# New cost table for a static order, and the scale matmuls' tile: from a corner of the scores' tile to the transposes' PSUM pool

## The chip, the cores and the metric

The kernel runs on one core of a Trainium2 chip. The metric is the device time of one execution in microseconds (us), the median of several runs. All engines of the core take part: TensorE (PE, matmuls), VectorE (DVE), ScalarE (ACT), GpSimd (POOL) and SyncE (SP, which here only issues DMAs).

## The reference

Attention on q, k, v of shape (4 batches, 8 heads, 576 positions, 64), and a mixture of four experts on what it gives:

```python
scores = q @ k.T / sqrt(64)
scores = where(scores >= max(scores) - tau, scores, -1e9)      # tau = 0.02
attn   = softmax(scores) @ v                                   # per batch and head
x      = attn.transpose(0, 2, 1, 3).reshape(2304, 512)
p      = domain_probs / (domain_probs.sum(-1) + 1e-9)
out    = sum over e of p[:, e] * (relu(x @ w1[e]) @ w2[e])     # w1: 512x1024, w2: 1024x512
```

Inputs and output are float32. Nearly all products are taken as three float16 products (high by high, high by low, low by high), for which each operand is scaled by a power of two and split in two.

## The kernel before, in words

**Attention.** One item is a pair of heads of one batch (`g`) and one block `j` of 128 query rows (`j` = 4 is the 64 rows left over). There are 80 items, 20 for each batch. An item's path: PE writes the scores S of two heads (`emit_qk`, L909 and L915 or L921); DVE copies them with the row's maximum (L968), ACT takes the exponential (L991), POOL the threshold (L983), DVE applies it and sums (L1000). In batch 0 the result is turned on PE (ET, L1020, L1049). In batches 1 to 3 ACT and DVE split it in two float16 parts (L1119, L1125) and SP issues DMA transposes (L1082). Then PE multiplies with V (av, L1232 to L1246), and ACT and DVE write the block X of the experts' input (L1277, L1288).

**Experts.** Experts 0 and 1 run beside the attention. As soon as a block X is there, units of it follow: first layer (L1348), relu and split (ACT L1360 and L1368, POOL L1375), second layer (L1390), result to `acc` (L1407, L1415). Their place in the order of priority is last (1000 and more), so that they fill PE where the attention has nothing ready. Experts 2 and 3 follow in a second stage, with seven products in place of eight (L1584, L1604 to L1632, L1664, L1682). Their weights are prepared from priority 500 on.

**Scales.** Each power of two comes from sums of squares (`squares`, on ACT or DVE), one small matmul with a matrix of ones that adds them over the partitions and spreads the sum (`total`, L453), and five DVE steps on its result (`pow2`, L467 to L486). The matmul's target `au` comes from `chain_tile`: below priority 999 one of two 128-column corners (`am0`, `am1`) of the tile `s_all`, three PSUM banks in which the scores also lie. Columns 704 to 960, the corners, are in the same bank as columns 512 to 576 and 960 to 1024, which belong to the scores. `total` is called for the queries and keys of each pair of heads of batches 1 to 3 (`t_bound`, 12 times), for V of each batch (`v_prep`, 4) and for the weights of experts 0 and 1 (`w_prep`, 2 and 4): 22 in all; the second stage's 8 have tiles of their own (QA).

**Pool `ma`.** Two PSUM tiles of one bank. ET, rp (the reciprocals' spread, batch 0 alone) and av take tiles from it. Tiles of a pool are granted in the order in which they were first named.

**The order.** Nothing is reordered on the chip: each engine runs its instructions in the order in which they were emitted, and `Plan` (L22 to L219) writes that order down while the kernel is built. It plays the program with a cost in ns for each operation, a latency from engine to engine (`LAT`), a delay until a freed tile can be taken (`FREED`), costs for DMAs, and a model of PE's two clocks, and at each moment gives a free engine the ready operation of lowest priority number. The costs set nothing but this order: a cost that is too long puts what depends on it later in its engine's queue than the chip would need. A dependency, also one between two uses of one bank of a tile, becomes a semaphore wait.

Of the kernel before, what the change touches and what calls it, by code (L numbers as in the profile page):

```python
# [21 lines left out]
class Plan:  # L22
# [6 lines left out]
    LAT = {  # L29
        ("PE", "PE"): 0, ("PE", "ACT"): 230, ("DVE", "ACT"): 198, ("ACT", "DVE"): 145,  # L30
        ("PE", "DVE"): 200, ("POOL", "DVE"): 50, ("ACT", "POOL"): 200, ("SP", "PE"): 0,
        ("SP", "ACT"): 0, ("SP", "DVE"): 0, ("SP", "POOL"): 0, ("POOL", "SP"): 70,
    }
    GAP, FILL = 400, 3000
    WINDOW, WARMUP = 3413.0, 4000.0
    warm, cold, work, window, pe_end = True, 0.0, 1e9, 0, 0.0
    FREED, LANES = 150, 8
    START, DONE, HELD = 625, 1000, 877

    def __init__(self):  # L40
        self.ops, self.writer, self.readers = [], {}, {}
        self.slots, self.kinds, self.order, self.users = {}, {}, {}, {}
        self.tiles = {}

# [29 lines left out]
    def reserve(self, u):  # L74
        pool = self.kinds[u[0]][0]
        s = (pool, u)
        if s not in self.users:
            self.users[s] = 0
            self.order[pool].append(u)
        return s  # L80
# [20 lines left out]
    def schedule(self):  # L101
        n = len(self.ops)
# [15 lines left out]
        at = [0.0] * n  # L118
# [17 lines left out]

        now, seq = 0.0, 0
        while True:
            progress = True
            while progress:  # L140
                progress = False
                for e in engines:
                    if free[e] > now:
                        continue
                    skipped = []
                    pick = None
                    h = ready[e]
# [12 lines left out]
                    for u in use:  # L160
                        if u not in granted:
                            pool = self.kinds[u[0]][0]
                            granted.add(u)
                            avail[pool] -= 1
                            head[pool] += 1
# [62 lines left out]
def topk_attention_moe_kernel(  # L228
# [201 lines left out]
    def squares(n, dst, src, junk, r, w, use, prio, on_dve=False):  # L430
        if on_dve:
# [9 lines left out]
        act(  # L441
            n / 0.96 + 200,
            lambda: nc.scalar.activation(
# [6 lines left out]
    def total(n, au, src, r, w, use, prio):  # L450
        pe(
            300,
            lambda: nc.tensor.matmul(pl.t(*au)[:, 0:n], ones, src(), start=True, stop=True),  # L453
# [5 lines left out]
    def pow2(src, s_out, p_out, r, w, use, prio, tmp, au, add=None):  # L459
# [3 lines left out]
        def step(fn, rr, ww, more=()):  # L463
            dve(195, fn, rr, ww, use=use + list(more), prio=prio)

# [179 lines left out]
    def t_turn(g, prio):  # L645
# [12 lines left out]
        for c, n, u in ((0, 1024, ru), (8, 256, tl)):  # L658
            act(
                n / 1.1 + 200,  # L660
                lambda c=c: nc.scalar.activation(
# [4 lines left out]
            dve(  # L666
                n / 0.84 + 80,
                lambda c=c: nc.vector.scalar_tensor_tensor(
# [280 lines left out]
    def item(i):  # L949
# [11 lines left out]
        pe(  # L961
            (1300 if j < 4 else 1150) - 300 * (g >= NP * T32), lambda: emit_qk(pl.t(*su), pl.t(*T), j),
            [("T", g)] if g >= NP * T32 else [("T", g, c) for c in (0, 1024)], [("S", i)], use=[su, T], prio=i,
        )
        for h in heads:

            def cm(h=h):
# [7 lines left out]
            o = dve(  # L975
                890, cm, [("S", i), "tc"] + [("qf", g)] * (g >= NP * T32), [("ss", i, h), ("m", i, h)], use=[su, ssu, mu], prio=i,
            )
        if SK(i) == "S0":
            b_users.append(o)
        for h in heads:  # L980
            gp(
                470,
                lambda h=h: nc.gpsimd.tensor_scalar(  # L983
# [14 lines left out]
            dve(  # L998
                930,
                lambda h=h, col=col: nc.vector.scalar_tensor_tensor(  # L1000
# [14 lines left out]
        for h in heads:  # L1015
# [15 lines left out]
            for hh in range(2 if j == 4 else 0):  # L1031
# [5 lines left out]
            pe(  # L1037
                470, tr, [("E", i, h), "ident"], [("et", i, h)], use=[au, eu], prio=i + 0.2,
            )
# [46 lines left out]
    def spread(i, c0):  # L1086
# [5 lines left out]
        def rec():  # L1092
# [6 lines left out]
        dve(  # L1099
            391, rec, [("ri", i, h) for h in heads], [("ri", i)], use=[ru], prio=i + 0.2,  # L1100
        )
# [13 lines left out]
        for h in heads:  # L1115
# [7 lines left out]
            def lo(h=h):  # L1123
# [6 lines left out]
            act(  # L1130
                767 if j < 4 else 1100, hi, [("E", i, h), ("ri", i)], [("eh", i, h)],
                use=[eu, fu, ru], prio=i + 0.2,
            )
            dve(
                824 if j < 4 else 1159, lo, [("E", i, h), ("ri", i), ("eh", i, h)],
                [("el", i, h)], use=[eu, fu, ru], prio=i + 0.2,
# [20 lines left out]
    def group(gi):  # L1157
# [115 lines left out]
        for Xu, c0, o, c, jj in dest:  # L1273
            key = ("x", Xu, b, jj, pr)
            act(
                c / 1.2 + 210,
                lambda Xu=Xu, c0=c0, o=o, c=c: nc.scalar.activation(  # L1277
# [43 lines left out]
    def unit(name, Xu, xkeys, c0, tiles, u, first, last):  # L1321
# [16 lines left out]
        for f in range(f0, f1):  # L1338
# [3 lines left out]
            def g1(mu=mu, W=W):  # L1342
# [15 lines left out]
            act(  # L1358
                {256: 467, 128: 364}[n],
                lambda mu=mu, hru=hru, f=f: nc.scalar.activation(  # L1360
# [12 lines left out]
            gp(  # L1373
                {256: 850, 128: 536}[n],
                lambda hu=hu, hru=hru: nc.gpsimd.tensor_tensor(  # L1375
# [5 lines left out]
        for i, t in enumerate(tiles):  # L1381
# [22 lines left out]
            if first:  # L1404
                act(
                    571,
                    lambda ou=ou, acc=acc, s=s: nc.scalar.activation(  # L1407
# [121 lines left out]
    def unit7(name, xs, m, tiles, u, last):  # L1529
# [5 lines left out]
        for j in range(2):  # L1535
# [3 lines left out]
            gp(  # L1539
                267,  # L1540
                lambda j=j: nc.gpsimd.tensor_scalar(  # L1541
# [27 lines left out]
        for k in range(4):  # L1569
# [6 lines left out]
            def product(r, a, b, reg=reg, pu=pu, P=P, q=q, k=k):  # L1576
# [19 lines left out]
                pe(  # L1596
                    6 * (m / 2.4 + 4.4), go, [("wq", e, k, wk), ("wl", e, k, wk)] + xk,
                    [("p", r) + q], use=[pu(r), P] + xu, prio=1000 + n_moe,
# [130 lines left out]
    with tc.manual_schedule():  # L1729
# [163 lines left out]
```

## Time and profile before

| | us |
|---|---|
| time, median of 3 runs | 1007.48 (1006.35 to 1007.99) |
| the profiled execution's own time | 1011.84 |
| its span, first to last instruction | 1010.1 |
| PE busy | 951.2 (94% of the span) |
| DVE busy | 730.9 (72%) |
| ACT busy | 555.7 (55%) |
| POOL busy | 251.0 (25%) |
| mean granted TensorE clock | 0.979 of full speed |

The attention runs to about 575 us, beside experts 0 and 1; the first products of expert 2 begin near 640 us. Times in the rows below are us from the span's start unless marked ns. "L968" is line 968 of the kernel. What stands in brackets with an arrow is the idle time of the engine just before the group, and what ended it. SPq and PEld are SP's queue and PE's weight loads.

### The profile page before, as it was taken

What the parts mean: (1) busy time and instruction counts of PE and PEld (TensorE: products, weight loads), DVE (VectorE), ACT (ScalarE), POOL (GpSimd) and SP (SyncE); (2) the same over time, 40 slices, a digit from 0 to 9 for tenths busy, and PEclk for the clock granted to TensorE, in tenths of its full rate; (3) what the DMA queues carried; (4) which work ended last, traced back from release to release, by engine and by line L of the source; (5) the groups of instructions that cost most, each with busy time, mean ns of one, the idle gap of its engine ahead of it and who ended that gap; (6) DMA issues with size and microseconds to landing.
All of it is one profiled execution on the core that took longest, in us unless ns stands there. A gap on an engine that the chain in (4) does not pass through costs nothing.

```text
span 1010.1 us, 20161 instructions
## 1 busy us (share of the span) xinstructions
PE 951.2 (94%) x7472; PEld 617.8 (61%) x7472; DVE 730.9 (72%) x1826; ACT 555.7 (55%) x1177; POOL 251.0 (25%) x401
## 2 busy tenths in 40 slices
PE   7689899999956999999999999998999999999998
PEld 4466556566624567665666667765766667666663
DVE  3887778798887988768777563988865578755551
ACT  3888786676855768775666668743322223322220
POOL 1226364344513335434234234200000000000000
PEclk9799999999978999999999999998999999999999
DMA  8803165756689764778574515310120111101101
GB/s 189 240 12 95 43 134 149 142 105 129 119 170 190 123 112 102 136 164 137 94 148 92 118 64 189 100 37 22 53 74 1 45 61 37 49 2 53 32 2 42
DMA packets 243234, 95.99 MB, mean 95 GB/s; under 512 B 209600, under 2 KB 230080, under 8 KB 243136
## 3 DMA queue, kind: packets, MB, share of 16 engines
q1 hardware_dynamic: 241024, 94.18, 42.1%
q8 instruction: 58, 0.95, 0.4%
q10 hardware_dynamic: 2112, 0.52, 0.3%
q14 instruction: 40, 0.33, 0.1%
HBM read 40.41 MB, written 14.16 MB: 54 GB/s over the span
## 4 chain that ended last, share of the span: by engine, by line
PE 82%; DMA 6%; DVE 4%; ACT 4%; SPq 2%; issue 1%; ACTq 0%; POOL 0%; DVEq 0%
PE mm L1664 18%; PE Q L1584 17%; PE mm L1390 16%; PE mm L1348 15%; PE av L1232 5%; PE S L909 5%; DMA PT<-E 4%; DMA T<-R 2%; SPq L424 2%; PE av L1241 1%; PE S L915 1%; PE ET L1020 1%; ACT W L816 1%; DVE SS L968 1%; SPq L1082 1%
## 5 line engine op out<-in xcount | busy, mean ns | idle before, releaser
L1664 PE MATMUL mm<-WP,h 128*128 128x512 f16 x864 | 218.3, 379 | 0.0
L1390 PE MATMUL mm<-W,h 128*128 128x512 f16 x864 | 204.4, 379 | 0.0
L1584 PEld LDWEIGHTS <-WP 128*128 128x128 f16 x1680 | 154.7, 99 | 63.9 <-issue 4.2
L1348 PEld LDWEIGHTS <-W 128*128 128x128 f16 x2016 | 174.0, 98 | 30.4 <-issue 3.1
L1348 PE MATMUL mm<-X,W 128*128 128x256 f16 (+1 forms) x1632 | 180.5, 266 | 1.7 <-ACT hr L1360 0.9
L1604 DVE SCALAR_TENSOR_TENSOR qt<-Q,wc,qt 128x256 f32<-128x256 f32 (+1 forms) x280 | 123.5, 454 | 77.5 <-PE Q L1584 73.5
L1625 ACT ACTIVATE h<-qt 128x256 f16<-128x256 f32 (+1 forms) x160 | 62.1, 394 | 198.6 <-DVE qt L1604 198.2
L1375 POOL TENSOR_TENSOR h<-hr,h 128x256 f16<-128x256 f32 (+1 forms) x168 | 125.8, 756 | 117.2 <-ACT h L1368 68.9
L991 ACT ACTIVATE E<-SS,sm 128x576 f32<-128x576 f32 x144 | 108.9, 770 | 44.4 <-DVE SS L968 29.1
L1000 DVE SCALAR_TENSOR_TENSOR E<-SS,sm,E 128x576 f32<-128x576 f32 x144 | 121.9, 860 | 15.3 <-ACT E L991 10.0
L1390 PEld LDWEIGHTS <-h 128*128 128x128 f16 x864 | 82.0, 99 | 78.2 <-issue 0.4
L983 POOL TENSOR_SCALAR sm<-sm,tau_p 128x1 f32<-128x1 f32 x144 | 71.0, 494 | 194.3 <-DVE SS L968 138.8
L1664 PEld LDWEIGHTS <-h 128*128 128x128 f16 x864 | 82.9, 98 | 59.5
L1584 PE MATMUL Q<-T,WP 128*128 128x256 f16 (+1 forms) x960 | 117.0, 263 | 0.0
L968 DVE TENSOR_SCALAR_CACHE_REDUCE SS<-S,qc 128x576 f32<-128x576 f32 x108 | 86.5, 810 | 27.2 <-DMA PT<-E 12.7
L1125 DVE SCALAR_TENSOR_TENSOR E<-E,ri,E 128x576 f16<-128x576 f32 (+1 forms) x120 | 91.7, 792 | 12.0 <-ACT E L1119 11.5
L1119 ACT ACTIVATE E<-E,ri 128x576 f16<-128x576 f32 (+1 forms) x120 | 82.8, 722 | 23.0 <-DMA PT<-E 6.4
L1360 ACT ACTIVATE hr<-mm,wc 128x256 f32<-128x256 f32 (+1 forms) x168 | 72.9, 438 | 39.9 <-PE mm L1348 35.0
L1584 PE MATMUL Q<-X,WP 128*128 128x256 f16 (+1 forms) x720 | 90.6, 265 | 3.8 <-ACT qt L1614 3.8
L909 PE MATMUL S<-T 64*128 64x512 f16 (+3 forms) x440 | 76.8, 451 | 12.4 <-DVE SS L968 12.2
L1541 POOL TENSOR_SCALAR psc<-pnv,wpm 128x2 f32<-128x2 f32 (+1 forms) x20 | 8.2, 415 | 295.1 <-DVE acc L1682 249.5
L1232 PE MATMUL av<-PT,V 128*64 128x320 f16 (+3 forms) x768 | 65.3, 312 | 13.2 <-DMA PT<-E 12.6
(140 smaller groups left out, 1001.1 us busy)
## 6 DMA issues: line engine op xcount, KB each, us to landing
wraw<-in_moe_w_dram SPq DMA_DIRECT2D x64, 256.0 KB, 3.4
part<-acc SPq DMA_DIRECT2D x18, 256.0 KB, 2.3
X<-x_dram SPq DMA_DIRECT2D x9, 512.0 KB, 3.6
acc<-part SPq DMA_DIRECT2D x18, 256.0 KB, 3.4
raw<-in_q_dram SPq DMA_DIRECT2D x32, 128.0 KB, 3.0
out_dram<-acc SPq DMA_DIRECT2D x16, 256.0 KB, 2.2
raw<-in_k_dram SPq DMA_DIRECT2D x28, 128.0 KB, 3.1
x_dram<-X SPq DMA_DIRECT2D x7, 512.0 KB, 3.8
```

Source lines behind the costliest of these rows:

```text
L909: nc.tensor.matmul(ps[:, 1024 * h:1024 * h + SM] if j < 4 else ps[rows(h), 0:SM], qm(h, a), km(h, c), start=(y == 0), stop=(y == last),)
L968: nc.vector.tensor_scalar(out=pl.t(*ssu)[:, S * h:S * h + S], in0=pl.t(*su)[:, 960 * h:960 * h + S], scalar1=qc[:, g, 2:3] if g >= NP * T3 ...
L991: lambda h=h: nc.scalar.activation(out=pl.t(*eu)[:, S * h:S * h + S], in_=pl.t(*ssu)[:, S * h:S * h + S], func=ACTF.Exp, scale=-1.0, bias= ...
L1000: lambda h=h, col=col: nc.vector.scalar_tensor_tensor(out=pl.t(*eu)[:, S * h:S * h + S], in0=pl.t(*ssu)[:, S * h:S * h + S], scalar=pl.t(* ...
L1125: nc.vector.scalar_tensor_tensor(out=o, in0=e, scalar=pl.t(*ru)[:, h:h + 1], in1=hh, op0=ALU.mult, op1=ALU.subtract,)
L1232: nc.tensor.matmul(av[64 * h:64 * h + 64, 0:n], va(slice(0, 128), vp, 4 * h + c), ts(slice(0, 128), tp, 5 * h + c, 0, n), start=(c == 0 an ...
L1348: nc.tensor.matmul(ps[:, 0:n], w[:, wp, 0, c * 128:(c + 1) * 128], x[:, c, xp, c0:c0 + n], start=(i == 0), stop=(i == len(seq) - 1),)
L1375: lambda hu=hu, hru=hru: nc.gpsimd.tensor_tensor(out=pl.t(*hu)[:, 1, 0:n], in0=pl.t(*hru)[:, 0:n], in1=pl.t(*hu)[:, 0, 0:n], op=ALU.subtra ...
L1390: nc.tensor.matmul(ps, h[:, hp, 128 * i:128 * i + 128], w[:, wp, 1, :], start=(f == f0 and hp == 0 and wp == 0), stop=(f == f1 - 1 and hp ...
L1584: nc.tensor.matmul(reg(r), w[:, wp, o:o + 128], xb(b, c, xp), start=(n == 0), stop=(n == 5),)
L1604: lambda: nc.vector.scalar_tensor_tensor(out=tmp(o), in0=reg(r), scalar=wcs, in1=tmp(i), op0=ALU.mult, op1=ALU.add),
L1664: nc.tensor.matmul(ps, ht()[:, hp, 128 * i:128 * i + 128], w[:, wp, o:o + 512], start=(f == 0 and hp == 0 and wp == 0), stop=(f == NF - 1 ...
```

## The change

`chain_tile` gives a tile AM of the pool `ma` from priority 5 on (before: from 999 on); three of the 22 calls, V of batch 0 and the two of expert 0's weights, are below 5 and keep the corner, 19 move. AM is `loose`: it takes any free tile of the pool and has no place in the pool's order. In `Plan`, an engine is free again a `TAIL` before an operation's end (on PE the result is there 160 ns after the engine is free), most latencies are shorter, a freed tile can be taken after 55 ns, and many single costs are new. `v_prep` of batch 0 is moved from priority 1.5 to 2.5. No instruction is added or taken away. The core of the diff:

```diff
     LAT = {
-        ("PE", "PE"): 0, ("PE", "ACT"): 230, ("DVE", "ACT"): 198, ("ACT", "DVE"): 145,
-        ("PE", "DVE"): 200, ("POOL", "DVE"): 50, ("ACT", "POOL"): 200, ("SP", "PE"): 0,
+        ("PE", "PE"): -160, ("PE", "ACT"): 60, ("DVE", "ACT"): 45, ("ACT", "DVE"): 60,
+        ("PE", "DVE"): 40, ("POOL", "DVE"): 60, ("ACT", "POOL"): 85, ("SP", "PE"): 0,
         ("SP", "ACT"): 0, ("SP", "DVE"): 0, ("SP", "POOL"): 0, ("POOL", "SP"): 70,
+        ("DVE", "POOL"): 100, ("ACT", "SP"): 30, ("DVE", "SP"): 30, ("DVE", "PE"): 55,
+        ("ACT", "PE"): 55, ("DVE", "DVE"): 40, ("ACT", "ACT"): 40, ("POOL", "POOL"): 60,
     }
+    TAIL = {"PE": 160, "ACT": 102, "DVE": 83, "POOL": 20, "SP": 0}
-    FREED, LANES = 150, 8
+    FREED, LANES = 55, 8
...
+                if u[0] in self.loose:
+                    if avail[pool] < 1:
+                        return False
+                    continue
...
-                    end = now + ns
-                    free[e] = end
+                    end = now + ns + (self.TAIL[e] if e == "PE" else 0)
+                    free[e] = end - self.TAIL[e]
...
-                    lat = self.LAT.get((e, self.ops[j][0]), 150)
+                    lat = self.LAT.get((e, self.ops[j][0]), 60)
...
     kind("AM", "ma", "ma", [128, 512], FP32)
+    pl.loose.add("AM")
 
     def chain_tile(key, prio):
         nonlocal n_am
-        if prio >= 999:
+        if prio >= 5:
             return ("AM", key)
...
-        at(0, v_prep, 0, v_load(0, -36), 1.5)
+        at(0, v_prep, 0, v_load(0, -36), 2.5)
```

Costs of single operations, in ns:

| operation | before | after |
|---|---|---|
| total, L453 | 300 | 180 |
| one step of pow2, L467 to L486 | 195 | 150 |
| scores, batch 0 (j = 4), L909 | 1300 (1150) | 1384 (1030) |
| scores, batches 1 to 3 (j = 4), L909 | 1000 (850) | 932 (856) |
| copy and maximum, DVE L968 | 890 | 820 |
| threshold, POOL L983 | 470 | 508 |
| selection, DVE L1000 | 930 | 872 |
| low part, DVE L1125 (j = 4) | 824 (1159) | 850 (1036) |
| high part, ACT L1119 (j = 4) | 767 (1100) | 765 (1005) |
| low part of h, POOL L1375, 256 (128) columns | 850 (536) | 830 (515) |
| factors of the second stage, POOL L1541 | 267 | 470 |
| product, PE L1584 | 6 (m / 2.4 + 4.4) | 6 (m / 2.4 + 2.5) |

The costs of some ten more operations change by less than 0.15 us each. The costs of the first and second layer (L1348, L1390) and all the constants of DMAs stay.

## Rows read from the trace of the kernel before

**Rows 1.** Busy time of each engine in stretches, granted clock, DMA share, GB/s (cut).
```profile
0.00:76.00 76.00, 56.95 (x419) 37.87 (x420) 51.74 (x164) 52.84 (x103) 17.90 (x42) 0.91 0.58 146
76.00:278.00 202.00, 193.52 (x1563) 121.15 (x1562) 164.96 (x433) 151.66 (x330) 93.68 (x131) 0.99 0.55 115
278.00:329.00 51.00, 32.05 (x261) 18.65 (x260) 39.59 (x102) 28.86 (x55) 11.81 (x23) 0.83 0.90 180
...
404.00:480.00 76.00, 72.00 (x584) 46.16 (x584) 57.52 (x141) 51.20 (x103) 29.23 (x46) 1.00 0.79 145
480.00:682.00 202.00, 201.40 (x1644) 134.68 (x1639) 144.20 (x338) 134.48 (x272) 58.95 (x86) 1.00 0.44 105
682.00:707.00 25.00, 21.18 (x136) 14.24 (x135) 20.14 (x52) 9.49 (x18) 2.06 (x4) 0.86 0.07 22
...
985.00:1010.00 25.00, 21.07 (x98) 9.38 (x96) 4.18 (x6) 0.03 (x1) 0.00 (x0) 0.98 0.11 42
```

**Rows 2.** Timeline of PE from 286 to 311 us (cut).
```profile
286.83 1.65 PE L1232 MATMUL av<-PT,V 128*64 128x320 f16 x21 [0.81 <-DMA PT<-E]
...
292.69 1.46 PE L909 MATMUL S<-T 64*128 64x512 f16 x6 [3.66 <-DVE SS L968]
...
298.84 1.46 PE L909 MATMUL S<-T 64*128 64x512 f16 x6 [4.25 <-DVE SS L968]
...
306.27 3.09 PE L1232 MATMUL av<-PT,V 128*64 128x320 f16 x21 [0.80 <-DMA PT<-E]
...
309.83 0.82 PE L909 MATMUL S<-T 64*128 64x512 f16 x6
```

**Rows 3.** Timeline of DVE from 277 to 286 us (cut).
```profile
277.04 0.81 DVE L968 TENSOR_SCALAR_CACHE_REDUCE SS<-S,qc 128x576 f32<-128x576 f32 x1
277.78 0.08 DVE L968 DVE_READ_ACCUMULATOR SS<-S,qc 128x1 f32 x1
277.78 0.81 DVE L1000 SCALAR_TENSOR_TENSOR E<-SS,sm,E 128x576 f32<-128x576 f32 x1
278.52 0.08 DVE L1000 DVE_READ_ACCUMULATOR E<-SS,sm,E 128x1 f32 x1
...
281.45 0.82 DVE L968 TENSOR_SCALAR_CACHE_REDUCE SS<-S,qc 128x576 f32<-128x576 f32 x1 [0.79 <-PE S L453]
...
284.08 1.54 DVE L1125 SCALAR_TENSOR_TENSOR E<-E,ri,E 128x576 f16<-128x576 f32 x2
```

**Rows 4.** Timeline of ACT, 277 to 279 us (cut).
```profile
277.89 0.78 ACT L991 ACTIVATE E<-SS,sm 128x576 f32<-128x576 f32 x1 [0.23 <-DVE SS L968]
```

**Rows 5.** Timeline of SP's queue, 277 to 331 us: first and last of 27 groups.
```profile
277.14 3.31 SPq L676 DMA_TRANSPOSE T<-R  x1
...
330.87 0.58 SPq L424 DMA_DIRECT2D raw<-in_k_dram  x1
```

**Rows 6.** Who waited for whom: us in total, times, longest us.
```profile
DVE SS L968 <- PE S L453: 6.4, 7, 1.8
PE av L1232 <- DMA PT<-E: 12.6, 13, 2.3
PE S L909 <- DVE SS L968: 12.2, 6, 4.3
```

**Rows 7.** Instructions of single lines: duration ns min/median/max.
```profile
L983 POOL TENSOR_SCALAR sm<-sm,tau_p x144: 257/268/1244, 16.6 to 559.7; 128x1 f32<-128x1 f32 x144
```

**Rows 8.** One line's DMAs: issue to landing, us min/median/max (L1082).
```profile
DMA to landing us min/median/max: 2.3/3.3/5.9
```

**Rows 9.** Groups by line and shape: busy us, mean ns of one.
```profile
L434 DVE SCALAR_TENSOR_TENSOR junk<-V 128x576 f16<-128x576 f32 x4 | 3.0, 757 | 0.1
```

**Rows 10.** Timeline of PE, 33 to 34 and 692 to 693 us (cut).
```profile
33.79 1.12 PE L1020 MATMUL ET<-ident,E 128*128 128x128 f32 x4 [1.92 <-ACT rb L1216]
...
692.89 2.90 PE L1584 MATMUL Q<-X,WP 128*128 128x256 f16 x12 [3.79 <-ACT qt L1614]
```

More of the change, by code (lines that the diff above doesn't have):

```diff
@@ L42, in __init__ @@
         self.slots, self.kinds, self.order, self.users = {}, {}, {}, {}
-        self.tiles = {}
+        self.tiles, self.loose = {}, set()
     def pool(self, name, n):
@@ L78, in reserve @@
             self.users[s] = 0
-            self.order[pool].append(u)
+            if u[0] not in self.loose:
+                self.order[pool].append(u)
         return s
@@ L164, in schedule @@
                             avail[pool] -= 1
-                            head[pool] += 1
+                            head[pool] += u[0] not in self.loose
                     if e == "SP":
@@ L441, in squares @@
         act(
-            n / 0.96 + 200,
+            n / 0.96 + 180,
             lambda: nc.scalar.activation(
@@ L451, in total @@
         pe(
-            300,
+            180,
             lambda: nc.tensor.matmul(pl.t(*au)[:, 0:n], ones, src(), start=True, stop=True),
@@ L463, in step @@
         def step(fn, rr, ww, more=()):
-            dve(195, fn, rr, ww, use=use + list(more), prio=prio)
+            dve(150, fn, rr, ww, use=use + list(more), prio=prio)
         if add:
@@ L659, in t_turn @@
             act(
-                n / 1.1 + 200,
+                n / 1.17 + 270,
                 lambda c=c: nc.scalar.activation(
@@ L666, in t_turn @@
             dve(
-                n / 0.84 + 80,
+                n / 0.84 + 130 + 50 * (n < 600),
                 lambda c=c: nc.vector.scalar_tensor_tensor(
@@ L961, in item @@
         pe(
-            (1300 if j < 4 else 1150) - 300 * (g >= NP * T32), lambda: emit_qk(pl.t(*su), pl.t(*T), j),
+            ((1384 if j < 4 else 1030) if g < NP * T32 else (932 if j < 4 else 856)), lambda: emit_qk(pl.t(*su), pl.t(*T), j),
             [("T", g)] if g >= NP * T32 else [("T", g, c) for c in (0, 1024)], [("S", i)], use=[su, T], prio=i,
@@ L975, in item @@
             o = dve(
-                890, cm, [("S", i), "tc"] + [("qf", g)] * (g >= NP * T32), [("ss", i, h), ("m", i, h)], use=[su, ssu, mu], prio=i,
+                820, cm, [("S", i), "tc"] + [("qf", g)] * (g >= NP * T32), [("ss", i, h), ("m", i, h)], use=[su, ssu, mu], prio=i,
             )
@@ L981, in item @@
             gp(
-                470,
+                508,
                 lambda h=h: nc.gpsimd.tensor_scalar(
@@ L998, in item @@
             dve(
-                930,
+                872,
                 lambda h=h, col=col: nc.vector.scalar_tensor_tensor(
@@ L1037, in item @@
             pe(
-                470, tr, [("E", i, h), "ident"], [("et", i, h)], use=[au, eu], prio=i + 0.2,
+                445, tr, [("E", i, h), "ident"], [("et", i, h)], use=[au, eu], prio=i + 0.2,
             )
@@ L1099, in spread @@
         dve(
-            391, rec, [("ri", i, h) for h in heads], [("ri", i)], use=[ru], prio=i + 0.2,
+            405, rec, [("ri", i, h) for h in heads], [("ri", i)], use=[ru], prio=i + 0.2,
         )
@@ L1130, in spread @@
             act(
-                767 if j < 4 else 1100, hi, [("E", i, h), ("ri", i)], [("eh", i, h)],
+                765 if j < 4 else 1005, hi, [("E", i, h), ("ri", i)], [("eh", i, h)],
                 use=[eu, fu, ru], prio=i + 0.2,
@@ L1134, in spread @@
             dve(
-                824 if j < 4 else 1159, lo, [("E", i, h), ("ri", i), ("eh", i, h)],
+                850 if j < 4 else 1036, lo, [("E", i, h), ("ri", i), ("eh", i, h)],
                 [("el", i, h)], use=[eu, fu, ru], prio=i + 0.2,
@@ L1275, in group @@
             act(
-                c / 1.2 + 210,
+                c / 1.2 + 168,
                 lambda Xu=Xu, c0=c0, o=o, c=c: nc.scalar.activation(
@@ L1358, in unit @@
             act(
-                {256: 467, 128: 364}[n],
+                {256: 467, 128: 365}[n],
                 lambda mu=mu, hru=hru, f=f: nc.scalar.activation(
@@ L1373, in unit @@
             gp(
-                {256: 850, 128: 536}[n],
+                {256: 830, 128: 515}[n],
                 lambda hu=hu, hru=hru: nc.gpsimd.tensor_tensor(
@@ L1405, in unit @@
                 act(
-                    571,
+                    683,
                     lambda ou=ou, acc=acc, s=s: nc.scalar.activation(
@@ L1539, in unit7 @@
             gp(
-                267,
+                470,
                 lambda j=j: nc.gpsimd.tensor_scalar(
@@ L1596, in product @@
                 pe(
-                    6 * (m / 2.4 + 4.4), go, [("wq", e, k, wk), ("wl", e, k, wk)] + xk,
+                    6 * (m / 2.4 + 2.5), go, [("wq", e, k, wk), ("wl", e, k, wk)] + xk,
                     [("p", r) + q], use=[pu(r), P] + xu, prio=1000 + n_moe,
```

## The prediction

> **What bounds the kernel now.** I read the stretches first [rows 1]. PE is busy for 951.2 of 1010.1 us, so nothing that leaves PE's work as it is can give back more than the 58.8 us in which PE stands idle, and what the low clock costs. No instruction is added or taken away, so PE's work stays. The idle time lies in few places: 19.05 us up to 76 us, 8.48 us from 76 to 278, 18.95 us from 278 to 329, 4.0 us from 404 to 480, 0.6 us to 682, 3.82 us from 682 to 707 and 3.93 us at the end; the two stretches that were left out (329 to 404 and 707 to 985) have none. Wherever PE is at 100%, a faster DVE, a shorter wait or another order is worth nothing by itself.
>
> Next I read the largest hole in PE's timeline [rows 2]. From 286 to 310 us not one product of an expert runs: what was ready of experts 0 and 1 has been used up, and PE has only the attention, which comes as fast as DVE and SP's queue deliver it (waits of 3.66 and 4.25 us for DVE's L968, others for DMAs). In the hole the granted clock falls (0.83 of full speed as a mean of the stretch, so 1.2 GHz for part of it), and the same six score matmuls take 1.46 us in place of 0.82. So this hole is paid for by an attention that was too slow before it: each us by which the blocks X of batch 1 come earlier closes one.
>
> Was the attention bound by an engine there? From 76 to 278 us DVE, the busiest engine after PE, is busy for 164.96 of 202 us [rows 1]: 37.0 us idle. It was not saturated. What it waited for is partly the order itself, which comes next.
>
> **The change part by part.** *Costs of the order.* With the old table an L968 holds DVE for 890 ns, an L1000 for 930 and an L1125 for 824. The rows show 0.74, 0.74 and 0.77 us from one start to the next [rows 3]. The new table minus its tail of 83 ns gives 737, 789 and 767. Per head the old order believed in 351 ns too much (153 + 141 + 57); a batch has 36 heads, so 12.6 us per batch. The latencies were off in the same direction: from DVE to ACT the old table has 198 ns and the new one 45, and L991 starts 0.03 us after L968's last instruction ends (277.78 + 0.08 to 277.89) [rows 3, 4]. With such a table the scores, av and transposes were put late in their queues, and PE took experts' work ahead of them. The new order puts them some 13 us per batch earlier, as far as the other queues follow. Before the hole lie batch 1 and the later part of batch 0, about one batch and a half, so an estimated 12.6 x 1.5 = 19 us of lateness stands against a hole of 18.95 us. I don't take all of it: one group of the filler, three to twelve matmuls, can't be interrupted, and SP's queue is nearly full there (below). I take two thirds, 12.6 us, with bounds of 0 and 18.95. With it goes the low clock: two groups of scores at 1.46 in place of 0.82 and one av at 3.09 in place of 1.65 make 2.7 us [rows 2]; two thirds are 1.8 us (0 to 2.7).
>
> *The other holes.* Of the 8.48 us from 76 to 278 and the 4.0 us from 404 to 480 I take a quarter and a half, 2 us each (0 to 8.5, 0 to 4.0): the same lateness, but part of it is batch 0, which has no filler yet.
>
> *The corner.* 19 of 22 totals leave the scores' bank. In it a total had to stand between two items: L968 waited 0.79 us at 281.45 for a matmul L453 whose columns it doesn't read [rows 3]; all such waits are 6.4 us in 7 times on DVE [rows 6]. DVE isn't the bound, so these are no term of their own; they are part of what lets the attention come earlier (bounds 0 to 6.4, already in the 12.6). The pool has two tiles, and an av keeps one for its 1.65 to 3.09 us of matmuls [rows 2] and the readings after them; a total needs one only until the first of pow2's steps. Nine of the 19 fall into batch 0, where ET turns over both tiles; if each held up an ET by the 0.5 us that it needs it, that is 4.5 us on ACT's and PE's chain, most of it behind filler. I take 0 (-4.5 to 0).
>
> *`v_prep` of batch 0, one item later.* It issues four DVE squares (757 ns each, 3.0 us in all) [rows 9], one total, the five steps of pow2, three POOL operations; its DMAs keep their place. DVE gains 3 us early for the items. But L1216 needs its scale before it frees the tile of rp, and PE has waited 1.92 us for that at 33.79 [rows 10]. Later scale, later ET, and no filler exists to cover it. I take 0 for the first stretch, with bounds of -5 and +5.
>
> *Second stage.* It is PE at 100% but for the 3.79 us at 692.89, where the products then run at half speed [rows 10]: a chain through the last weights' raw buffers, DMA, squares and QA. The new order may move it either way; I take 0 (-5 to +6).
>
> *New waits.* A table without slack puts a score or an av at the head of PE's queue at the moment at which it should be ready. What comes late on the chip now stops PE, with filler standing behind it; the old table had up to 0.2 us of reserve in each step. The transposes land 2.3 to 5.9 us after their issue, median 3.3 [rows 8], and the threshold, one column per partition, takes 257 to 1244 ns [rows 7]. So far such waits on PE are 12.6 us for transposes and 12.2 us for L968 [rows 6], mostly in the holes. Bounds: 0, if filler that is ready covers them as before, and 36 us, if each of the 24 av of batches 1 to 3 waits for the 1.0 us from least to median landing and each of their 60 scores 0.2 us. I take 5 us, near the end of the rows, which show hardly any outside the holes.
>
> **The sum.** 12.6 + 1.8 + 2 + 2 + 0 + 0 - 5 = 13.4 us saved. From the profiled execution, 1011.84, that is 998.4. That execution is 4.4 us above the median of the runs; from the median, 1007.48, it is 994.1. I forecast **994 us**.
>
> **The rivals.** *A, SP's queue is the bound of the hole.* From 277.14 to 331.45 SP issues for 52.3 us (the sum of its 27 groups) [rows 5]: transposes of the queries and keys of batch 2, transposes of probabilities, loads. Then no order of DVE or PE gets batch 1's last groups through faster, and only the small terms are left: 2 + 2 us, so 1003.5 (1000 to 1008). For it: in this stretch the DMA share is 0.90, and PE waits there for transposes. Against it: from 76 to 278 us the share is 0.55, so the queue is full because work was bunched there, not because it is too much over a batch.
>
> *B, PE stops in its own order: slower.* The place is the score and av matmuls of batches 1 to 3, 60 + 24. What the better table saves (18.4 us) is lost again once the mean wait in front of these 84 exceeds 0.22 us. At the upper bound but for a few, 30 us, the time is 1007.5 - 18.4 + 30 = 1019 (1010 to 1030). For it: the spread of landings and of the threshold, against latencies cut to 30 to 100 ns. Against it: from 480 to 682 us, where the last items of batch 3 run, PE idles for 0.6 us in all [rows 1], and a score that is a little late still stands behind a group of filler. The Trainium skill (SBUF — State Buffer, Who interferes with whom) says that a DVE instruction with two inputs in SBUF and a GpSimd instruction that reads SBUF exclude each other, the later one standing still for the whole of the other. The trace agrees: the threshold's longest run is 976 ns above its median, about one L1000. By that rule a denser DVE makes more thresholds late; if that cost PE a whole L1000 (0.81 us) at 36 of the 60 items, 29 us, it would be this rival's time, and by the median of the trace it is nothing.
>
> *C, all holes from 76 to 682 us close.* 8.48 + 18.95 + 4.0 + 0.6 + 2.7 = 34.7 us less at most; less a few us of waits, 978 (973 to 985). For it: DVE idles for 37.0 us before the hole, twice what it would have to catch up. Against it: batch 0 has little filler, since its first blocks X come only with its first av.
>
> **How the numbers follow.** Chances: forecast 0.50 (own range 986 to 1002), A 0.17, B 0.24, C 0.09. From 1007.5, 0.2% is 2 us, about what a measurement of this kernel tells from no change. Faster: 0.47 of the forecast's 0.50, 0.08 of A's, all of C's, so 0.64. Same: 0.02 + 0.08 + 0.02 (B's low edge) = 0.12. Slower: 0.01 + 0.01 + 0.22 = 0.24. The range is 977 to 1012: about 0.04 of C lies below and 0.14 of B above.
>
> **What would show it.** Right: PE idle from about 270 to 330 us under 8 us and the clock there at full speed; the attention's last threshold (559.7 us before [rows 7]) at least 25 us earlier, and a longer stretch of pure expert work behind it; no L968 waiting for L453 after 70 us. Waits of PE for L968 and for transposes outside the holes of 5 us in sum. A would show as a hole of the old size with SP's queue full; B as many waits of 0.3 to 1 us in front of L909 and L1232 with PE idle all over 100 to 560 us. The forecast is wrong if PE's idle sum stays above 55 us or falls under 35.

## The result and the profile after

The changed kernel takes 1000.1 us (median of 11 runs, 998.34 to 1002.9), the kernel before 1008.68 (11 runs, 1006.35 to 1015.67): a ratio of 0.9911, 95% interval 0.9891 to 0.9932. 994 had been forecast, in a range of 977 to 1012. The profiled execution of after took 999.85 us, 12.0 less than that of before (1011.84), which lay 3.2 us above its median. So the traces have 12.0 us to explain, the medians 8.6.

The page of after, span, busy time and granted clock in 40 slices:

```profile
span 998.1 us, 20163 instructions
...
PE 947.9 (95%) x7472; PEld 614.1 (62%) x7472; DVE 736.0 (74%) x1826; ACT 558.0 (56%) x1177; POOL 249.9 (25%) x401
...
PEclk9899999999999999999999999999999999999999
```

PE stands idle for 50.2 us (998.1 - 947.9), before for 58.9 (1010.1 - 951.2). Its busy time fell by 3.3 us with the same 7472 instructions, and the mean granted clock rose from 0.979 to 0.993. Idle and busy time together, 8.7 + 3.3 make the 12.0. The stretches of after (window, its length, then busy us of PE, PEld, DVE, ACT, POOL; granted clock, DMA share, GB/s), beside [rows 1]:

```profile
0.00:76.00 76.00, 54.87 (x397) 35.21 (x397) 50.48 (x159) 51.95 (x102) 17.05 (x43) 0.93 0.59 146
76.00:278.00 202.00, 191.40 (x1585) 118.74 (x1584) 178.09 (x468) 156.78 (x337) 91.84 (x130) 1.00 0.60 124
278.00:329.00 51.00, 48.11 (x378) 29.39 (x377) 46.13 (x110) 36.16 (x70) 17.30 (x32) 0.97 0.93 183
329.00:404.00 75.00, 70.75 (x710) 47.10 (x709) 65.58 (x179) 58.41 (x131) 34.50 (x54) 1.00 0.73 129
404.00:480.00 76.00, 71.94 (x606) 44.49 (x606) 69.83 (x168) 53.81 (x102) 28.77 (x46) 1.00 0.80 156
480.00:682.00 202.00, 198.90 (x1578) 135.51 (x1577) 133.22 (x308) 128.65 (x265) 54.84 (x82) 1.00 0.34 87
682.00:707.00 25.00, 25.00 (x173) 16.69 (x171) 18.10 (x42) 5.17 (x13) 0.94 (x2) 1.00 0.13 44
```

The stretch from 329 to 404 us in the kernel before, which [rows 1] leaves out:

```profile
329.00:404.00 75.00, 75.00 (x726) 48.37 (x724) 64.80 (x167) 55.88 (x126) 31.82 (x56) 1.00 0.63 111
```

Length minus PE's busy time is PE's idle time. The hole from 278 to 329 us went from 18.95 to 2.89, the stall after 682 from 3.82 to 0. Elsewhere it grew: 2.1 us up to 76, 2.1 from 76 to 278, 4.25 from 329 to 404, 2.5 from 480 to 682. PE's timeline in what had been the hole, beside [rows 2]:

```profile
284.11 0.82 PE L918 MATMUL S<-T 64*128 64x512 f16 x6 [0.70 <-DVE SS L977]
...
285.05 5.99 PE L1399 MATMUL mm<-W,h 128*128 128x512 f16 x27
291.20 0.82 PE L918 MATMUL S<-T 64*128 64x512 f16 x6 [0.16 <-DVE SS L977]
...
296.73 0.82 PE L918 MATMUL S<-T 64*128 64x512 f16 x6
...
298.31 1.47 PE L1357 MATMUL mm<-X,W 128*128 128x256 f16 x12
...
308.31 2.14 PE L1241 MATMUL av<-PT,V 128*64 128x256 f16 x22 [1.39 <-DMA PT<-E]
```

L918, L1241, L1357 and L1399 are the L909, L1232, L1348 and L1390 of before. Now products of experts stand between the scores. The score matmuls take 0.82 us, and at 298.31 first-layer products from batch 1's last block X begin, which came at 310.76 before. The last part of this block, as DVE writes it, in the kernel before and in the one after:

```profile
311.48 0.42 DVE L1288 SCALAR_TENSOR_TENSOR X<-av,X 128x256 f16<-128x256 f32 x1
```
```profile
296.59 0.42 DVE L1297 SCALAR_TENSOR_TENSOR X<-av,X 128x256 f16<-128x256 f32 x1
```

I call this start X1, the end of batch 1. It came 14.9 us earlier, and 16.06 us of the hole went.

### The profile page after: what moved, and what is told of

Same layout as the page of the kernel before. It is cut to its first block, busy times and chain, and to the rows that moved or that the text cites. A ratio compares the mean times of both kernels' runs of the same rounds, so it can differ in the third digit from the quotient of the medians.

```text
span 998.1 us, 20163 instructions
## 1 busy us (share of the span) xinstructions
PE 947.9 (95%) x7472; PEld 614.1 (62%) x7472; DVE 736.0 (74%) x1826; ACT 558.0 (56%) x1177; POOL 249.9 (25%) x401
## 4 chain that ended last, share of the span: by engine, by line
PE 54%; DVE 17%; DMA 8%; ACT 7%; issue 4%; POOL 1%; SPq 0%; DVEq 0%; ACTq 0%; POOLq 0%
PE mm L1673 17%; PE Q L1593 16%; PE mm L1399 8%; PE mm L1357 7%; DMA PT<-E 5%; DVE SS L977 4%; DVE E L1009 4%; DVE E L1134 3%; PE av L1241 2%; PE S L918 2%; DMA T<-R 2%; DVE R L677 1%; ACT E L1000 1%; ACT E L1128 1%; ACT hr L1369 1%
## 5 line engine op out<-in xcount | busy, mean ns | idle before, releaser
L1673 PE MATMUL mm<-WP,h 128*128 128x512 f16 x864 | 221.7, 379 | 0.0
L1399 PE MATMUL mm<-W,h 128*128 128x512 f16 x864 | 206.9, 379 | 1.5 <-ACT hr L1369 1.1
L1357 PEld LDWEIGHTS <-W 128*128 128x128 f16 x2016 | 174.4, 98 | 36.4 <-issue 6.8
L1357 PE MATMUL mm<-X,W 128*128 128x256 f16 (+1 forms) x1632 | 182.1, 267 | 4.3 <-ACT hr L1369 3.7
L1384 POOL TENSOR_TENSOR h<-hr,h 128x256 f16<-128x256 f32 (+1 forms) x168 | 131.7, 790 | 126.6 <-ACT h L1377 108.4
L1000 ACT ACTIVATE E<-SS,sm 128x576 f32<-128x576 f32 x144 | 109.8, 771 | 49.8 <-DVE SS L977 29.7
L1399 PEld LDWEIGHTS <-h 128*128 128x128 f16 x864 | 81.8, 99 | 77.6 <-issue 3.3
L992 POOL TENSOR_SCALAR sm<-sm,tau_p 128x1 f32<-128x1 f32 x144 | 66.8, 464 | 191.1 <-DVE SS L977 128.5
L1134 DVE SCALAR_TENSOR_TENSOR E<-E,ri,E 128x576 f16<-128x576 f32 (+1 forms) x120 | 93.8, 811 | 9.4 <-ACT E L1128 8.7
L977 DVE TENSOR_SCALAR_CACHE_REDUCE SS<-S,qc 128x576 f32<-128x576 f32 x108 | 86.0, 809 | 9.6 <-DMA PT<-E 4.2
L918 PE MATMUL S<-T 64*128 64x512 f16 (+3 forms) x440 | 75.4, 443 | 11.3 <-DVE SS L977 10.7
L1641 DVE SCALAR_TENSOR_TENSOR h<-qt,h 128x256 f16<-128x256 f32 (+1 forms) x160 | 61.6, 395 | 29.6 <-ACT h L1634 26.9
```

The lines of the kernel that those rows point to most:

```text
L918: nc.tensor.matmul(ps[:, 1024 * h:1024 * h + SM] if j < 4 else ps[rows(h), 0:SM], qm(h, a), km(h, c), start=(y == 0), stop=(y == last),)
L977: nc.vector.tensor_scalar(out=pl.t(*ssu)[:, S * h:S * h + S], in0=pl.t(*su)[:, 960 * h:960 * h + S], scalar1=qc[:, g, 2:3] if g >= NP * T3 ...
L1000: lambda h=h: nc.scalar.activation(out=pl.t(*eu)[:, S * h:S * h + S], in_=pl.t(*ssu)[:, S * h:S * h + S], func=ACTF.Exp, scale=-1.0, bias= ...
L1134: nc.vector.scalar_tensor_tensor(out=o, in0=e, scalar=pl.t(*ru)[:, h:h + 1], in1=hh, op0=ALU.mult, op1=ALU.subtract,)
L1357: nc.tensor.matmul(ps[:, 0:n], w[:, wp, 0, c * 128:(c + 1) * 128], x[:, c, xp, c0:c0 + n], start=(i == 0), stop=(i == len(seq) - 1),)
L1384: lambda hu=hu, hru=hru: nc.gpsimd.tensor_tensor(out=pl.t(*hu)[:, 1, 0:n], in0=pl.t(*hru)[:, 0:n], in1=pl.t(*hu)[:, 0, 0:n], op=ALU.subtra ...
```

## The experiments

All ratios are to the kernel before, timed beside it, with 95% intervals. "The hole" is PE's idle time from 278 to 329 us.

**The tile alone.** The old costs and latencies, totals in the pool `ma`.

```diff
         # kernel before
-        if prio >= 999:
+        if prio >= 5:        # and AM loose, as in the change
```

> The kernel before with the tile's move alone: AM, loose, from priority 5 on, the old cost table, v_prep at 1.5. Theory T (the new table's costs give the gain, by an attention that is put earlier): ratio to the kernel before 0.996 to 1.003, the hole around 280 to 330 us stays with over 12 us of PE idle, last threshold (L983's) not more than 10 us earlier than 559.7. Rival M (the move off the scores' bank gives it): 0.989 to 0.994, hole under 8 us. Rival O (any other order would move the time as much): anything from 0.99 to 1.01.

1.0061 (1.0035 to 1.0087): no gain. Two stretches of it:

```profile
76.00:278.00 202.00, 186.90 (x1490) 115.32 (x1489) 160.15 (x436) 148.99 (x321) 81.86 (x124) 0.97 0.56 114
278.00:329.00 51.00, 41.24 (x301) 24.50 (x300) 37.08 (x88) 29.95 (x59) 15.65 (x28) 0.84 0.85 168
```

The hole is 9.76 us, under the 12 of theory T, but 15.1 us lie idle before it (8.48 in the kernel before): the idle time moved to an earlier place.

**The change without the tile.**

```diff
         # kernel after
-        if prio >= 5:
+        if prio >= 999:
```

> The changed kernel with the corner kept below priority 999, everything else new. T: 0.989 to 0.995, last threshold within 10 us of the changed kernel's (about 516 us). M: 0.997 to 1.003. O: anything from 0.99 to 1.01. In both cases DVE's L977 waits again for single matmuls of the totals (5 to 10 us in sum).

0.9895 (0.9862 to 0.9928), as the whole change. Of the 6.4 us that DVE had waited for totals in the scores' bank [rows 6], here is what is left, where 5 to 10 had been expected:

```profile
DVE SS L977 <- PE S L462: 0.5, 2, 0.3
```

With the new costs DVE hardly meets such a total, corner or not. The tile move is worth nothing that the runs show; the gain is in the table.

**How much a mere other order is worth.** `FREED` changed by 10 ns, which means nothing on the chip, in the kernels before and after.

```diff
-    FREED, LANES = 150, 8   # kernel before
+    FREED, LANES = 160, 8
-    FREED, LANES = 55, 8    # kernel after
+    FREED, LANES = 65, 8
```

> The kernel before with FREED at 160 in place of 150: no information in it, but another order on every engine. T and M: within 0.4% of the kernel before. O: more than 0.6% away on either side.

> The changed kernel with FREED at 65 in place of 55: again only another draw of the order. T and M: 0.987 to 0.995 of the kernel before, last threshold 506 to 530 us. O: 0.996 or more.

1.0048 (1.0025 to 1.0072) and 0.9891 (0.9859 to 0.9924). A nudge without meaning moved one kernel by half a per cent, more than theory T's 0.4% and less than O's 0.6%, and the other by 0.2%. So e1's 0.6% is hardly more than chance in the order. The 0.9% of the change is more: the three orders with all of its table and latencies up to here (after, e2, e4) gave 0.9911, 0.9895 and 0.9891.

**Costs or latencies.** First the change with the old latencies and `FREED`, tails only on ACT, DVE and POOL. Then the tile with the new latencies and old costs.

```diff
         # kernel after: LAT, its default and FREED as in the kernel before
-    TAIL = {"PE": 160, "ACT": 102, "DVE": 83, "POOL": 20, "SP": 0}
+    TAIL = {"PE": 0, "ACT": 102, "DVE": 83, "POOL": 20, "SP": 0}
         # e1: LAT and its default as in the kernel after, but without PE's tail in it
+        ("PE", "PE"): 0, ("PE", "ACT"): 220, ("PE", "DVE"): 200,
-    FREED, LANES = 150, 8
+    FREED, LANES = 55, 8
```

> The changed kernel's costs of operations and the tails of ACT, DVE and POOL, but the old latencies (198, 145, 230, default 150, FREED 150, no tail on PE): DVE's load in the plan is right, each handover has 0.1 to 0.15 us of reserve. Theory T1 (the load that the plan gives DVE is what moved the attention; short latencies only add stalls): 0.984 to 0.992, last threshold under 535 us, PE's gaps before scores (L918) under 5 us from 76 to 640. T2 (the latencies do it, since an item's chain is long): 0.996 or more, last threshold over 545 us.

> e1 (old costs of operations, no tails, tile moved) with the new latencies and FREED 55 (PE's tail put into its latencies). T1: 0.998 to 1.008, near e1's 1.006, with a hole of over 10 us of PE idle before 330 us. T2: 0.988 to 0.995, last threshold under 535 us.

0.9859 (0.9839 to 0.9878) and 1.0043 (1.0023 to 1.0064). The whole gain comes with the costs and the tails (with which `v_prep`'s later place always goes here); the short latencies alone bring none, and with the old ones the kernel is faster than with the new. e5's stretches:

```profile
76.00:278.00 202.00, 187.29 (x1532) 116.84 (x1531) 171.18 (x459) 153.37 (x329) 87.75 (x127) 0.98 0.62 122
278.00:329.00 51.00, 44.15 (x376) 28.06 (x372) 41.56 (x98) 36.12 (x74) 21.15 (x32) 1.00 0.87 171
```

One mark of T1 failed: PE's waits for scores from 76 to 640 us are 9.8 us in e5, not under 5, and 8.8 in after.

**Is it DVE's three costs?** My step in the prediction, alone.

```diff
         # kernel before: L968, L1000, L1125
-                890   930   824 / 1159
+                737   789   767 / 1102
```

> The kernel before with three numbers of its table changed: copy and maximum 890 to 737, selection 930 to 789, low part 824 to 767 (j = 4: 1159 to 1102), as the starts of these operations lie in the trace; all else, tile and latencies too, is old. T1: these three are most of the 351 ns per head, so the hole from 278 to 329 us falls from 18.95 us of PE idle under 8, the last threshold comes 20 us or more earlier than 559.7, and the ratio is 0.990 to 0.996. T2: hole over 12 us, 0.997 to 1.004.

1.0007 (0.9993 to 1.002). The hole is still there:

```profile
278.00:329.00 51.00, 37.59 (x283) 21.24 (x281) 40.85 (x98) 30.75 (x59) 11.96 (x24) 0.83 0.88 182
```

13.4 us of it, at a clock of 0.83. DVE's three costs by themselves bring nothing, so my step was wrong or not enough.

**Which tail?** e5 with one tail taken away, of ACT, then of DVE: the planner believes that each instruction holds its engine 102 or 83 ns longer.

```diff
-    TAIL = {"PE": 0, "ACT": 102, "DVE": 83, "POOL": 20, "SP": 0}
+    TAIL = {"PE": 0, "ACT": 0, "DVE": 83, "POOL": 20, "SP": 0}     # e9
+    TAIL = {"PE": 0, "ACT": 102, "DVE": 0, "POOL": 20, "SP": 0}    # e10
```

> e5 (new costs and tails, old latencies, 0.986) with ACT's tail at 0 in place of 102: the plan holds ACT 102 ns too long for each operation. Theory D (what counts is the load that the plan gives DVE): 0.984 to 0.991, last threshold under 528 us. Rival A (ACT's load counts as much): 0.995 or more, last threshold over 540.

> e5 with DVE's tail at 0 in place of 83: the plan holds DVE 83 ns too long for each of its operations. D: 0.995 to 1.004, last threshold over 540 us, batch 1's last (item 39) over 288 against e5's 280.8. Rival A: 0.984 to 0.991. And the stall at 682 to 707 us comes back (3.6 to 3.9 us of PE idle) if the attention ends after some 545 us, as in all four kernels whose last threshold was at 556 or later; none whose last was at 538 or before had it.

Without ACT's tail 0.9982 (0.9965 to 0.9998): nearly all of e5's gain is gone, by one number. Without DVE's 0.9857 (0.9833 to 0.9881): nothing lost, though a head's three DVE operations are again 249 of my 351 ns too long in the plan (the other 102 stay corrected). Two smaller marks missed: e9's last threshold is at 530.7 us and not over 540, and e10's at 545.5 brings no stall after 682 us. The stretches and the last block X of batch 1, first without ACT's tail, then without DVE's:

```profile
278.00:329.00 51.00, 36.17 (x271) 20.84 (x271) 41.76 (x107) 30.15 (x56) 13.38 (x24) 0.83 0.91 182
...
312.34 0.42 DVE L1295 SCALAR_TENSOR_TENSOR X<-av,X 128x256 f16<-128x256 f32 x1
```
```profile
76.00:278.00 202.00, 184.48 (x1455) 112.10 (x1454) 168.35 (x443) 147.02 (x320) 81.16 (x123) 0.96 0.57 118
278.00:329.00 51.00, 48.32 (x416) 32.21 (x414) 42.11 (x103) 37.72 (x77) 23.28 (x36) 1.00 0.94 168
...
308.27 0.41 DVE L1295 SCALAR_TENSOR_TENSOR X<-av,X 128x256 f16<-128x256 f32 x1
```

Without ACT's tail the old hole is back, 14.83 us at 0.83, with X1 as late as in the kernel before. Without DVE's tail X1 is late too, but the idle time lies earlier, 17.5 us from 76 to 278, so that products of experts are left over for the place of the hole, which is 2.68 us. Part of e9's hole is such a move too, the other way: it idles 11.3 us from 76 to 278, e5 14.7. Over both stretches e9 idles 26.1 us and e5 21.6, so 4.6 of the 8.0 us between their holes are more idle time.

How the hole comes about without ACT's tail, on PE and on DVE:

```profile
292.64 0.82 PE L916 MATMUL S<-T 64*128 64x512 f16 x6
...
299.43 1.46 PE L916 MATMUL S<-T 64*128 64x512 f16 x6 [5.70 <-DVE SS L975]
```
```profile
295.95 1.28 DVE L675 SCALAR_TENSOR_TENSOR R<-raw,qc,R 128x1024 f16<-128x1024 f32 x1
297.16 0.48 DVE L675 SCALAR_TENSOR_TENSOR R<-tl,qc,R 128x256 f16<-128x256 f32 x1
...
297.83 0.80 DVE L975 TENSOR_SCALAR_CACHE_REDUCE SS<-S,qc 128x576 f32<-128x576 f32 x1
```

The scores written from 292.64 on are read at 297.83, behind two selections (L1007) and the preparation of batch 2's queries (L675) in DVE's queue, and the next scores need their place. No product of an expert runs on PE in e9 between 292.66 and 308.64. In e5 the same L675 stands in front of an L975 too (294.10 and 294.50), but there PE has 30 products of an expert to run meanwhile.

**Do reserves in the plan stop the new waits?** First in two places of after, then in all handovers between engines of e5, and e5 nudged by 10 ns.

```diff
         # e8: kernel after
-    START, DONE, HELD = 625, 1000, 877
+    START, DONE, HELD = 625, 1300, 877
-                        heapq.heappush(events, (now + self.FREED, 3, s[0]))
+                        heapq.heappush(events, (now + (400 if s[0] == "s" else self.FREED), 3, s[0]))
         # e12: e5
-    FREED, LANES = 150, 8
+    FREED, LANES = 250, 8
-                    lat = self.LAT.get((e, self.ops[j][0]), 150)
+                    lat = self.LAT.get((e, self.ops[j][0]), 150) + 100 * (e != self.ops[j][0])
         # e11: e5
-    FREED, LANES = 150, 8
+    FREED, LANES = 160, 8
```

> The changed kernel with reserve where PE stalls: in the plan the scores' tile can be taken 400 ns after its last reader in place of 55, and a DMA's landing costs 1300 ns in place of 1000. Rival B in small (the changed kernel's waits in front of scores and av, 9.3 and 4.6 us from 76 to 640, are lost time that a reserve gives back): 0.980 to 0.987, waits in front of L918 and L1241 under 5 us in sum. If filler is short anyway and the waits only move: 0.988 to 0.993.

> e5 with 100 ns more on each latency between two engines and FREED at 250: twice the reserve. If reserve helps because PE then waits less in its order: 0.979 to 0.987. If e5 stands near the best, the later attention takes it back: 0.987 to 0.995.

> e5 with FREED at 160 in place of 150: another draw of its order. If e5's lead over the four kernels with short latencies (0.9891 to 0.9911) comes from its reserve: 0.982 to 0.988. If it was a good draw: 0.988 to 0.992.

0.9897 (0.9876 to 0.9918), 0.9873 (0.985 to 0.9896) and 0.9827 (0.9804 to 0.985). A later DMA landing and a later score tile in the plan don't help: PE's waits for L977 are 17.1 us in e8. The old latencies are enough, another 100 ns bring nothing more. e11, 993.56 us, is the fastest kernel here and beats both; what sets it apart from e5 (0.9859) is one nudge, so that difference is luck. Its stretches:

```profile
278.00:329.00 51.00, 48.91 (x408) 30.35 (x405) 45.28 (x107) 37.15 (x75) 20.45 (x35) 0.97 0.96 186
329.00:404.00 75.00, 72.43 (x701) 47.24 (x699) 66.40 (x175) 59.08 (x134) 31.57 (x55) 1.00 0.69 128
404.00:480.00 76.00, 74.19 (x648) 47.20 (x645) 69.26 (x166) 54.31 (x103) 31.71 (x47) 1.00 0.80 155
480.00:682.00 202.00, 200.30 (x1593) 136.34 (x1591) 141.25 (x328) 127.82 (x265) 58.73 (x81) 1.00 0.37 89
```

From 329 to 682 us PE idles for 6.1 us (2.57 + 1.81 + 1.70), in after for 11.4.

**All kernels in one table.** Idle us of PE from the traces: from 76 to 329 us, of these the hole, and the late part, from the end of X1 to 640 us. The first six kernels have no tail on ACT in the plan, the others have it:

| | ratio | X1 | 76 to 329 | hole | late part | last threshold |
|---|---|---|---|---|---|---|
| before | 1 | 311.5 | 27.4 | 18.95 | 10.7 | 559.7 |
| e1 tile alone | 1.0061 | 319.4 | 24.9 | 9.8 | 4.9 | 562.0 |
| e3 before, nudged | 1.0048 | 315.1 | 30.5 | 18.1 | 7.2 | 559.0 |
| e6 tile, new latencies | 1.0043 | 315.9 | 30.4 | 16.6 | 7.6 | 556.4 |
| e7 three costs of DVE | 1.0007 | 316.3 | 28.9 | 13.4 | 8.0 | 537.8 |
| e9 e5 without ACT's tail | 0.9982 | 312.3 | 26.1 | 14.8 | 6.4 | 530.7 |
| after | 0.9911 | 296.6 | 13.5 | 2.9 | 13.1 | 516.2 |
| e8 after, reserves | 0.9897 | 299.6 | 20.3 | 6.8 | 12.9 | 518.7 |
| e2 after without tile | 0.9895 | 298.1 | 16.0 | 5.1 | 13.2 | 519.0 |
| e4 after, nudged | 0.9891 | 295.5 | 15.1 | 3.9 | 12.2 | 512.2 |
| e12 e5, more reserve | 0.9873 | 301.8 | 17.6 | 4.2 | 9.2 | 528.2 |
| e5 old latencies | 0.9859 | 301.3 | 21.6 | 6.9 | 7.6 | 518.2 |
| e10 e5 without DVE's tail | 0.9857 | 308.3 | 20.2 | 2.7 | 4.6 | 545.5 |
| e11 e5, nudged | 0.9827 | 298.4 | 15.9 | 2.1 | 8.0 | 517.1 |

## Why the prediction was right, and where it was not

**The hole.** Forecast -12.6 us, measured -16.06, because X1 comes 14.9 us earlier: an attention that comes earlier closed it, as forecast. In the table the hole goes with X1 but for e1 and e10, whose idle time lies earlier; the idle time from 76 to 329 us sorts all kernels, 24.9 to 30.5 us without ACT's tail and 13.5 to 21.6 with it. What failed is the step that named the cause: "Per head the old order believed in 351 ns too much (153 + 141 + 57); a batch has 36 heads, so 12.6 us per batch", DVE's operations. The size came out near by chance. e7 corrects just these and gains nothing, e10 spoils 249 of the 351 again and loses nothing, and e9 spoils ACT alone and loses the gain. The prediction has no term for ACT; its durations were right in the old table (770 ns for L991, 771 for the same line in after). But what e9 changes is how long an instruction holds its engine. Consecutive rows of ACT in after show that:

```profile
284.04 0.40 ACT L1377 ACTIVATE h<-hr 128x256 f16<-128x256 f32 x1
284.34 0.46 ACT L1369 ACTIVATE hr<-mm,wc 128x256 f32<-128x256 f32 x1
284.70 1.00 ACT L1128 ACTIVATE E<-E,ri 128x512 f16<-128x512 f32 x2
285.60 0.40 ACT L1377 ACTIVATE h<-hr 128x256 f16<-128x256 f32 x1
```

Each starts 0.10 us before the one ahead of it ends (284.04 + 0.40 to 284.34, and so on). The instructions that take part are these:

```profile
L1000 ACT ACTIVATE E<-SS,sm 128x576 f32<-128x576 f32 x144 | 109.8, 771 | 49.8 <-DVE SS L977 29.7 <-DVE ri L1103 17.8 <-DVE E L1134 2.1
L1128 ACT ACTIVATE E<-E,ri 128x576 f16<-128x576 f32 x96 | 71.4, 765 | 14.5 <-issue 5.0 <-DVE ri L1106 4.0 <-DMA T<-R 4.0
L1369 ACT ACTIVATE hr<-mm,wc 128x256 f32<-128x256 f32 x120 | 55.4, 464 | 22.8 <-PE mm L1357 22.1 <-POOL h L1384 0.2
L1377 ACT ACTIVATE h<-hr 128x256 f16<-128x256 f32 x120 | 48.9, 409 | 1.3
```

480 of them, by 0.10 us, are an estimated 48 us too much on ACT in the plan over some 500 us, about 12 per batch. DVE's too much per batch was 12.6 us, no less, and it isn't what moved the time: the size of an error in the table doesn't tell what it costs. ACT's tail alone, put into the kernel before, was not run, so it is shown that the gain needs it beside the new costs, not that it is enough. By which step a plan with a slower ACT delays X1 was not tested. The rows of e9 show only the end of it: scores that stand unread behind other work in DVE's queue while no product of an expert runs on PE. The write to this block just before X1 comes as early in e9 as in e5 (283.62 and 283.33 us), so nearly all of the 11 us by which X1 is later arise in the hole itself. The kernel before was late by then already (290.61, after 279.19): ACT's tail alone doesn't account for that part. e9 and e5 are one order each, but 1.2% apart, over twice what any nudge did.

**The low clock.** Forecast -1.8 us; PE's busy time fell by 3.3. The hole's clock rose from 0.83 to 0.97, and that of the stretch after 682 us from 0.86 to 1.00. The clock isn't all of it: e5's PE is busy for 944.7 us, 3.2 less than in after, at a mean clock of 0.988 against 0.993. Why the busy time differs between orders at a like clock stays open.

**The other holes.** Forecast -2 from 76 to 278 and -2 from 404 to 480 us; measured +2.1 and +0.06. There I had seen the same lateness as in the hole; the new order took none of it away.

**New waits.** Forecast +5 us; after has 6.75 more idle us where there had been next to none (4.25 from 329 to 404, 2.5 from 480 to 682), and 9 with the stretch from 76 to 278. One of them is no matter of 0.2 us: a single product waits 3.67 us for ACT.

```profile
133.12 1.47 PE L1357 MATMUL mm<-X,W 128*128 128x256 f16 x12 [3.67 <-ACT hr L1369]
...
PE S L918 <- DVE SS L977: 10.7, 14, 1.9
PE av L1241 <- DMA PT<-E: 4.5, 5, 1.4
```

The waits for L977 became more and shorter (14 of at most 1.9 us, before 6 of up to 4.3 [rows 6]); those for transposes fell from 12.6 to 4.5. Rival B was right in kind, at under a third of its 30 us. In the late part of the table the idle time goes with the short latencies: 12.2 to 13.2 us in all four kernels that have them together with the new costs, 4.6 to 9.2 in the five with the old or longer ones. But most of this is a move: over the whole of 76 to 640 us after idles for 24.6 us and e5 for 25.5. Of the 4.7 us by which e5's trace is shorter, 3.2 are PE's busy time.

**Corner.** Forecast 0 of its own; the tile alone (e1, +0.6%) and the change without it (e2, 0.2% below after) are about what a nudge does. No L977 waits for a total after 70 us any more, and the runs show no gain from that.

**`v_prep` and the first stretch.** Forecast 0, measured +2.1, inside the bounds. The step wasn't tried alone, so what part of it `v_prep` has stays open.

**Second stage.** Forecast 0, measured -3.82 us idle and the half clock with it. The prediction had named the chain, raw buffers, DMA, squares and QA, but not that an earlier attention starts it earlier. The last weights are issued at these times, in the kernel before and in after:

```profile
683.88 0.93 SPq L424 DMA_DIRECT2D wraw<-in_moe_w_dram  x2
```
```profile
643.21 0.93 SPq L433 DMA_DIRECT2D wraw<-in_moe_w_dram  x2
```

SP's queue isn't what holds them up. In the kernel before SP stands still from 655.07 us on, until DVE's L1459 has read a raw buffer (the longest of these waits is this one):

```profile
SPq L424 <- DVE WP L1459: 52.7, 7, 28.7
```

The preparation of these weights (first L1452, L1461 in after) follows the attention's last threshold by 24.0 us (559.7) and 21.4 us (516.2):

```profile
583.74 1.15 ACT L1452 ACTIVATE WP<-wraw,wsc 128x1024 f16<-128x1024 f32 x1 [4.39 <-DVE wpow L486]
```
```profile
537.55 1.14 ACT L1461 ACTIVATE WP<-wraw,wsc 128x1024 f16<-128x1024 f32 x1
```

The stall of 3.6 to 3.9 us is in the four kernels whose last threshold comes at 556 us or later, and in none of the ten others (at most 0.34). I had treated as independent two stages of which the second's preparation waits for the first.

**The sum.** -16.06 + 2.12 + 4.25 + 0.06 + 2.50 + 2.08 - 3.82 + 0.14 (from 707 us on) = -8.7 us idle, -3.3 us busy: -12.0 in the traces, where I had -13.4. The forecast of 994 took it off the median of three runs, 1007.48, though the trace it was read from had run 4.4 us longer; against the medians 8.6 were saved. That the sum came near is partly luck, since its errors cancel: the hole, the clock and the second stage gave 3.5, 1.5 and 3.8 us more than forecast, the other holes, the new waits and the first stretch 6.2, 1.8 and 2.1 less.

**The other rivals.** A is wrong: from 277 to 331 us SP's queue still issues for 49.2 us (29 groups, before 52.3 in 27 [rows 5]), and the hole is closed. A queue that is this full was no limit. C is wrong: PE still idles for 24.9 us from 76 to 682 (10.6 + 2.89 + 4.25 + 4.06 + 3.1).

**The marks.** The hole under 8 us, the last threshold 43.5 us earlier, no L977 behind a total and idle time between 35 and 55 came. The clock in the hole came to 0.97, not quite full speed, and the waits for L977 and for transposes are 13.3 us from 76 to 640 (8.8 + 4.5), where 5 had been forecast. An early last threshold is a bad mark by itself: e7 and e9 have it at 537.8 and 530.7 us, over 20 us early, and the hole with it.

## What to carry to other kernels

In a table of costs for a static order, write down how long an instruction holds its engine (from start to start in rows that follow each other without a wait), not its duration, and do so for the engine that looks idle too. A little reserve in the handovers between engines did no harm here: the four kernels with ACT's tail and long handovers lie at 0.9827 to 0.9873, the four with short ones at 0.9891 to 0.9911, though PE's waits for scores did not get shorter (9.8 us in e5, 8.8 in after). Before you credit an edit with half a per cent in such a kernel, change a number that means nothing and see what that moves. And undo an edit's parts one at a time: here the tile's move was worth nothing that the runs show, and the three costs that I named as the cause brought nothing alone.

## What the runs showed of the hardware that was not expected

ACT's instructions follow each other 0.10 us before the end of the one ahead (rows above). DVE's do by 0.07 us: 277.04 + 0.81 against 277.78, 277.78 + 0.81 against 278.52 [rows 3].

The threshold on POOL, one column, spreads as much as before:

```profile
L992 POOL TENSOR_SCALAR sm<-sm,tau_p x144: 259/267/1323, 16.6 to 516.2; 128x1 f32<-128x1 f32 x144
```

DVE is busy for 178.09 us from 76 to 278 us, 13 more than before, and yet the median stays at 267 ns and the longest is 1.3 us. A denser DVE did not make rival B's price. It would have taken 36 whole waits of 0.8 us in front of PE, and PE's wait for scores is 10.7 us in all.

The prediction read the longest threshold as the price of about one L1000. The trace of the kernel before shows another neighbour:

```profile
69.15 1.24 POOL L983 TENSOR_SCALAR sm<-sm,tau_p 128x1 f32<-128x1 f32 x1
```
```profile
68.77 1.49 DVE L434 SCALAR_TENSOR_TENSOR W<-wraw 128x1024 f16<-128x1024 f32 x1
```

All thresholds of more than 1.05 us, five in the kernel before and four in after, run beside such a DVE instruction on 1024 columns, of 1.2 to 1.5 us (L434 and L668; L850 and L677 in after), and none beside an L1000 alone.
